# Value products over 64-key halves into two PSUM banks, and scores as three products of split queries and keys

## The chip, the cores and the metric

The kernel runs on one core of one Trainium2 chip. The metric is the device time of one execution in microseconds (us), lower is better. Two kernels are told apart by medians of several executions of each on the same chip.

## What is computed

Inputs are q, k and v for 8 batches, 12 heads, 448 positions and 64 values per head, two 12x12 matrices that mix heads, and the weights of a gated feed-forward. All is float32.

```python
scores = scale * np.matmul(q, k.transpose(0, 1, 3, 2))
scores = np.einsum('bhij,hg->bgij', scores, w_pre)
scores = scores - np.max(scores, axis=-1, keepdims=True)
attn = np.exp(scores)
attn = attn / (np.sum(attn, axis=-1, keepdims=True) + 1e-09)
attn = np.einsum('bhij,hg->bgij', attn, w_post)
attn_out = np.matmul(attn, v)
# x = attn_out as 3584 rows of 768
h = (x @ w1) * (x @ w2) @ w3
out = h @ w_out
```

w_pre and w_post mix the twelve heads at each pair of positions, so scores of all heads have to stand side by side on partitions for the mixing, and the attention has to come back to one head at a time for the product with v.

## The kernel before

The attention of the eight batches runs in 360 steps: a step `n` stands for 10 query rows (`IB`) of a batch, 45 steps per batch (`NB`). All engines work through one program written in the order of the steps (the loop from L889); each engine takes its own instructions in that order, and every DMA is issued from SP's queue. In the order of a step:

- `do_later` (L927) issues the stores put off by the step before, after `fetch` (L926, even steps) has asked for mixed rows of scores; `load_kq` (L933) asks for queries and keys six steps ahead of their use.
- `largest` (even steps, DVE) takes the minimum of the mixed scores for `exp`; `scale` (odd steps) prepares w_post over the sums.
- `pieces` or `unit_pieces` (L950 to L960) convert float64 words of the weights to float32 pairs.
- `advance` (L968, L972) issues a share of the feed-forward's products (`e`, `eg`, `eo`), which fill TensorE between the attention's products.
- `exp` (even steps, ACT), then `av` (L974), `post` and `mix` (odd steps), and last one score unit, `qk` (L982).

**Scores** (`qk`, L166). A unit is a pair of heads `p` and 128 query rows `c` (two pairs and 64 rows each for c = 3). Two 64-row blocks times two heads make four products of 64 rows by 64 columns of weights with 448 keys moving, in float32. On the chip a float32 product is two matmul records. The four take the four quadrants of the array. The two PSUM banks (0 and 1) are copied by ACT (L179, L180) to `st` and stored to `raw_d`.

**Values** (`av`, L292). When 15 steps (150 query rows, the last time 148) of mixed attention stand in `mt`, six pairs of heads `g` are multiplied with v, three at a step and three two steps later. The 448 keys stand in four blocks (`NJ`) of 128; of the last block only 64 keys exist, and in `mt` the other half is zero: for every head, the first 5 of 10 query rows hold their 64 keys on the lower partitions and the other 5 on the upper. A product has 128 rows and 64 columns, two beside each other for the two heads. The result is gathered in bank 0 (`psa`); for batches from 2 on (`ONE`), ACT copies it to `xd` (L308) and it is stored to `x_d`. Batches 0 and 1 go another way (L321).

**Ends.** `ends` holds the closures that empty PSUM banks; `bank(i)` runs them before it hands out a bank that is still to be emptied. The score unit of the step uses banks 0 and 1 right after `post` and `mix`.

**Words.** `ask_words` (L96) loads words ahead into the pool `cs`, five buffers with tag `s` (`DEEP`), and `converting` (L132) uses one per piece: ACT squares it (L110), four DVE operations make float32 (L121 to L124), and in a later piece ACT and POOL split it in two parts (L129, L130), which are stored (L425). The first 40 words belong to a fold of two weights in batch 0, the next 32 to w1 and w2 around batch 1. In a piece the loads ahead are asked for first, then the current word is converted, then the one before is split. The same buffers serve `split` in `sums` (L483) later on.

Feed-forward products use parts of 128x128 weights in `fp32r`, which is one matmul record per product; three products (`PAIRS`) of high and low parts make one float32 product.

## Time and profile before

| what | us |
|---|---|
| median of 3 runs | 1441.87 |
| lowest and highest run | 1441.68 and 1443.87 |
| the profiled execution, whole | 1437.83 |
| its span, from the first instruction to the last | 1436.1 |

A busy TensorE is shown by PE and its weight loads by PEld; DVE, ACT, POOL and SP are the other engines. A row of a group gives operation, shapes, count, then busy us and the mean ns of one, then the idle time of the engine ahead of them. Matmuls are pipelined: one starts before the one before has ended, so their pace is read from start to start. A row of a timeline merges instructions of one line: start of the first, time from it to the end of the last, and their count.

### The profile page before, as it was taken

The numbers are of one execution on the slowest core, as the hardware profiler recorded it, in microseconds if no ns is written. First come the engines' busy times: TensorE is split into PE (matmuls) and PEld (weight loads), VectorE is DVE, ScalarE is ACT, GpSimd is POOL, SyncE is SP. The second block draws the span as 40 slices with busy tenths as digits, with TensorE's granted clock in tenths as the row PEclk, the third lists the DMA queues.
The fourth block names the chain that finished last, engine by engine and source line by source line (L and its number), as shares of the span: only waits on it lengthen the run. The fifth ranks groups of instructions, "written<-read, shape, count | busy, mean of one in ns | idle before, by whom it ended". The sixth has DMA issues, their size and how long they took to land.

```text
span 1436.1 us, 45775 instructions
## 1 busy us (share of the span) xinstructions
PE 1382.4 (96%) x18684; PEld 1055.2 (73%) x18684; DVE 741.1 (52%) x1497; ACT 832.4 (58%) x1952; POOL 620.3 (43%) x754
## 2 busy tenths in 40 slices
PE   5889999999999999999999999999999999999998
PEld 2457786776677667776777777777777777899988
DVE  6867566767544544432444436334444446345563
ACT  4867666777766666665656556556555445422231
POOL 2433233434433544532345336334335446446693
PEclk7989999999999999999999999999999999999999
DMA  8998789999999999999989979799879757698775
GB/s 294 366 326 279 236 270 322 320 312 317 324 286 348 355 356 330 362 346 349 287 275 290 320 259 280 249 323 354 288 229 281 241 177 223 195 337 270 231 232 171
DMA packets 203761, 416.87 MB, mean 290 GB/s; under 512 B 20528, under 2 KB 120112, under 8 KB 203472
## 3 DMA queue, kind: packets, MB, share of 16 engines
q1 hardware_dynamic: 203552, 413.94, 87.6%
q8 instruction: 149, 2.44, 0.7%
q14 instruction: 60, 0.49, 0.1%
HBM read 279.77 MB, written 134.09 MB: 288 GB/s over the span
## 4 chain that ended last, share of the span: by engine, by line
PE 82%; DMA 8%; DVE 4%; ACT 2%; issue 1%; POOL 1%; SPq 0%; DVEq 0%; POOLq 0%; ACTq 0%
PE e L702 21%; PE psa L301 11%; PE pso L260 10%; PE psm L220 9%; PE psq L174 7%; PE eg L522 5%; PE psf L360 4%; PE eo L553 4%; PE e2o L702 4%; PE e1o L702 4%; PE e3o L702 4%; DMA wu<-w_d 3%; DMA r<-raw_d 2%; DMA raw_d<-st 2%; ACT e L235 1%
## 5 line engine op out<-in xcount | busy, mean ns | idle before, releaser
L247 POOL TENSOR_SCALAR w<-wpo,ri 128x60 f32<-128x60 f32 x360 | 180.7, 518 | 485.1 <-DVE ri L245 465.3
L227 DVE TENSOR_REDUCE mn<-psm 128x1 f32<-128x448 f32 x360 | 207.7, 618 | 321.6 <-PE psm L220 321.3
L274 ACT COPY mt<-pso 128x480 f32<-128x480 f32 x352 | 197.9, 621 | 185.8 <-PE pso L260 185.6
L702 PE MATMUL e<-eh,wu 128*128 128x448 f32 x1008 | 296.8, 371 | 6.4 <-DVE c L656 3.2
L235 ACT ACTIVATE e<-psm,mn 128x448 f32<-128x448 f32 x360 | 226.8, 643 | 7.9 <-DVE mn L227 7.9
L702 PEld LDWEIGHTS e<-eh,wu 128*128 128x128 f32 x1008 | 187.5, 188 | 52.2 <-issue 26.8
L260 PEld LDWEIGHTS pso<-w,e 60*64 60x64 f32 x10080 | 175.2, 135 | 51.0 <-issue 42.5
L220 PE MATMUL psm<-r,wsc 60*64 60x448 f32 (+1 forms) x1440 | 191.2, 550 | 19.1 <-DVE cx L124 8.3
L260 PE MATMUL pso<-w,e 60*64 60x60 f32 x10080 | 199.1, 224 | 0.4 <-ACT mt L274 0.3
L702 PE MATMUL e<-el,wu 128*128 128x448 f32 x504 | 186.9, 371 | 0.0
L301 PE MATMUL psa<-mt,v 128*64 128x150 f32 (+1 forms) x2304 | 156.9, 292 | 4.1 <-ACT st L179 4.1
L301 PEld LDWEIGHTS psa<-mt,v 128*64 128x64 f32 x2304 | 143.6, 137 | 20.1 <-ACT st L179 6.7
L174 PE MATMUL psq<-kq 64*64 64x448 f32 x1176 | 154.6, 542 | 2.4 <-ACT st L179 2.4
L656 DVE TENSOR_TENSOR c<-c,e 128x448 f32<-128x448 f32 x168 | 101.7, 618 | 87.7 <-PE e L702 82.9
L179 ACT COPY st<-psq 128x448 f32<-128x448 f32 x162 | 86.4, 533 | 73.7 <-ACT mt L274 34.1
L522 PE MATMUL eg<-xh,wu 128*128 128x448 f32 x384 | 119.2, 381 | 6.3 <-DMA wu<-w_d 6.3
L641 POOL TENSOR_TENSOR el<-x,eh 128x448 fp32r<-128x448 f32 x90 | 103.7, 1170 | 32.8 <-ACT eh L640 29.9
L702 PEld LDWEIGHTS e<-el,wu 128*128 128x128 f32 x504 | 94.6, 188 | 22.5 <-issue 14.1
L174 PEld LDWEIGHTS psq<-kq 64*64 64x64 f32 x1176 | 60.8, 135 | 56.4 <-issue 28.8
L522 PEld LDWEIGHTS eg<-xh,wu 128*128 128x128 f32 x384 | 71.9, 190 | 38.7 <-issue 24.0
L244 DVE TENSOR_SCALAR sa<-sm 128x2 f32<-128x2 f32 x180 | 34.9, 194 | 113.6 <-ACT e L235 113.1
L180 ACT COPY st<-psq 128x448 f32<-128x448 f32 x162 | 87.6, 541 | 0.0
(99 smaller groups left out, 2010.1 us busy)
## 6 DMA issues: line engine op xcount, KB each, us to landing
r<-raw_d SPq DMA_DIRECT2D x344, 210.0 KB, 5.1
raw_d<-st SPq DMA_DIRECT2D x138, 448.0 KB, 6.1
wu<-w_d SPq DMA_DIRECT2D x104, 384.0 KB, 6.7
wu<-s_d SPq DMA_DIRECT2D x96, 384.0 KB, 4.8
wu<-w_d SPq DMA_DIRECT2D x51, 512.0 KB, 5.5
kq<-kq SPq DMA_DIRECT2D x42, 448.0 KB, 7.0
wu<-s_d SPq DMA_DIRECT2D x36, 512.0 KB, 4.9
x<-x_d SPq DMA_DIRECT2D x72, 224.0 KB, 5.7
```

Of the source, the lines that this page charges most:

```text
L174: nc.tensor.matmul(ps[s][z * PP:(z + 1) * PP], t[rows, q:q + PP], t[rows, k:k + S], start=True, stop=True)
L220: nc.tensor.matmul(ps[s][c * PP:(c + 1) * PP, :S], self.wsc[k], r[k, c], start=True, stop=True)
L227: self.nc.vector.tensor_reduce(mn[:, s:s + 1], self.psm[m][s][:, :S], axis=AX.X, op=ALU.min)
L235: nc.scalar.activation(e, p[:, :S], AF.Exp, bias=mn[:, s:s + 1], scale=-1.0, accum_out=sm[:, s:s + 1])
L247: nc.gpsimd.tensor_scalar_mul(w2[:, s], self.wpo, ri[:, s:s + 1])
L260: nc.tensor.matmul(self.pso[c][z * PP:(z + 1) * PP, at:at + HK], e[k, j * PP:(j + 1) * PP], w2s[k, s], start=True, stop=True)
L274: self.nc.scalar.copy(dst.rearrange("p j g (s i) -> p j s g i", s=2), src)
L301: nc.tensor.matmul(self.psa[rows, g % 3, :W], v[:, j, rows], mt[:, j, 2 * g + s, :W], start=(j == 0), stop=(j == NJ - 1))
L522: nc.tensor.matmul(p, u[:, k % (K1 // 2), x], xs[y][:, k], start=(k == 0 and t == 0), stop=(k == K1 - 1 and t == 2))
L641: nc.gpsimd.tensor_tensor(lo, x, hi.bitcast(F32), op=ALU.subtract)
L656: nc.vector.tensor_tensor(a[out], a[to[0]], p, op=ALU.add)
L702: nc.tensor.matmul(p, w[:, k, x], ops[m, k][y], start=(k == 0 and t == 0), stop=(k == nk - 1 and t == 2))
```

## The change

From batch 2 on, `av` takes keys in halves of 64: four products, two heads times two halves, stand in the four quadrants of the array, the halves going to banks 0 and 1. Of the last block each half is multiplied only with the query rows whose keys it holds (`halves`, half the columns). ACT copies bank 0 to `xd` and DVE adds bank 1.

From pair 2 of batch 2 on, `split_kq` makes a high and a low part of queries and keys (ACT `kh`, POOL `kl` in two halves), three steps before a pair's first unit. A score unit with c < 3 is then three products of parts per head, 64 rows by 128 columns in `fp32r`, six matmul records where there were eight. The unit with c = 3 stays as it was and moves ahead of its two pairs; both pairs' loads are asked for six steps before it.

The parts take memory: the pool of words is 3 buffers from the 41st word on, with two further buffers that live until the fold is over; `ask_words` then keeps 2 words asked for, not 5. `split` in `sums` uses 3 buffers. The host puts the last 64 query rows in front.

TensorE at the first score unit of batch 3, pair 0, before: `psm` are the mixed scores, `psq` the banks of the unit (the last figure but one is the head), `kq` queries and keys, `eg` a feed-forward product.

```order
L220 MATMUL psm43_0_4878<-r43_4697,wsc_138 64x448
L220 MATMUL psm43_1_4879<-r43_4697,wsc_138 64x448
L174 MATMUL psq3_0_0_0_4886<-kq3_0_4495 64x448
L174 MATMUL psq3_0_0_1_4887<-kq3_0_4495 64x448
L174 MATMUL psq3_0_0_0_4886<-kq3_0_4495 64x448
L174 MATMUL psq3_0_0_1_4887<-kq3_0_4495 64x448
L522 MATMUL eg0_4_1_4752<-xh0_1260,wu19_4729 128x448 x2
```

And after, `kh` and `kl` being the high and the low part:

```order
L242 MATMUL psm44_0_5020<-r44_4838,wsc_138 64x448
L242 MATMUL psm44_1_5021<-r44_4838,wsc_138 64x448
L189 MATMUL psq3_0_0_0_5028<-kh3_0_4866 128x448
L189 MATMUL psq3_0_0_1_5029<-kh3_0_4866 128x448
L189 MATMUL psq3_0_0_0_5028<-kl3_0_4867,kh3_0_4866 128x448
L189 MATMUL psq3_0_0_1_5029<-kl3_0_4867,kh3_0_4866 128x448
L189 MATMUL psq3_0_0_0_5028<-kh3_0_4866,kl3_0_4867 128x448
L189 MATMUL psq3_0_0_1_5029<-kh3_0_4866,kl3_0_4867 128x448
L563 MATMUL eg0_5_0_4965<-xl0_1261,wu20_4835 128x448
```

Four products of 64 output rows, two records each, became six of 128 output rows; the unit has stayed between the mixing and the feed-forward.

TensorE in the value products of batch 2, before (`mt` the attention, `v` a pair of heads):

```order
L301 MATMUL psa2_0_0_5984<-mt2_0_5258,v2_0_5280 64x150 x8
L301 MATMUL psa2_0_0_5984<-mt2_0_5258,v2_1_5282 64x150 x8
L301 MATMUL psa2_0_0_5984<-mt2_0_5258,v2_2_5284 64x150 x8
L260 MATMUL pso0_141<-w253_5885,e53_0_5864 64x60
L260 MATMUL pso1_142<-w253_5885,e53_0_5864 64x60
```

And after, the end of the first pair of heads and the start of the second; the last figure but one of `psa` is the bank:

```order
L333 MATMUL psa2_0_0_0_6074<-mt2_0_5318,v2_0_5342 64x150
L333 MATMUL psa2_0_0_1_6075<-mt2_0_5318,v2_0_5342 64x150
L341 MATMUL psa2_0_0_0_6074<-mt2_0_5318,v2_0_5342 64x15x5
L341 MATMUL psa2_0_0_1_6075<-mt2_0_5318,v2_0_5342 64x15x5
L341 MATMUL psa2_0_0_0_6074<-mt2_0_5318,v2_0_5342 64x15x5
L341 MATMUL psa2_0_0_1_6075<-mt2_0_5318,v2_0_5342 64x15x5
L333 MATMUL psa2_0_0_0_6074<-mt2_0_5318,v2_1_5344 64x150
L333 MATMUL psa2_0_0_1_6075<-mt2_0_5318,v2_1_5344 64x150
```

Eight products a pair became twelve over three blocks and four at half the columns for the last block.

The queue of SP in batch 1, where words of w1 and w2 are converted, before: `cs` is a load of words, `w_d` a store of a converted unit `wu`, `r` a fetch of scores, `raw2` a store of scores.

```order
L425 DMA w0_d_70<-wu13_4182 128x768
L103 DMA cs59_4215<-w2 128x3x256
L202 DMA r39_4273<-raw1_d_63 60x2x448 x2
L188 DMA raw2_d_64<-st2_4_2_4267 128x896
L425 DMA w1_d_71<-wu14_4270 128x768
L103 DMA cs60_4281<-w1 128x3x256
L425 DMA w1_d_71<-wu15_4308 128x768
L103 DMA cs61_4323<-w1 128x3x256
```

And after:

```order
L466 DMA w0_d_70<-wu13_4209 128x768
L105 DMA cs56_4242<-w1 128x3x256
L224 DMA r39_4302<-raw1_d_63 60x2x448 x2
L210 DMA raw2_d_64<-st2_4_1_4296 128x896
L466 DMA w1_d_71<-wu14_4299 128x768
L105 DMA cs57_4310<-w1 128x3x256
L466 DMA w1_d_71<-wu15_4342 128x768
L105 DMA cs58_4357<-w2 128x3x256
```

Behind the store of unit 13 word 59 was asked for, and now word 56. On ACT the squares (`cm`) of words stand as before, one per piece:

```order
L112 ACTIVATE cm55_4244<-cs55_4153 128x384
L296 COPY mt1_1_3780<-pso0_141 128x4x2x12x5
L296 COPY mt1_1_3780<-pso1_142 128x4x2x12x5
L201 COPY st2_4_1_4296<-psq2_4_1_0_4288 128x448
L202 COPY st2_4_1_4296<-psq2_4_1_1_4289 128x448
L131 CAST wu14_4299<-cx54_4157 128x3x128
L112 ACTIVATE cm56_4312<-cs56_4242 128x384
```

Word 56, which is asked for in the piece that squares word 55, is the next word that ACT takes.

The diff, its changed lines alone:

```diff
...
-DEEP = 5
+DEEP, KEPT = 5, 3
+PARTED = (2, 2)
...
-        while len(self.asked) < depth and self.sources:
+        while len(self.asked) < (depth if self.n_words < 5 * KF else KEPT - 1) and self.sources:
-            s = self.cs.tile([128, CW, 2], I32, tag="s", name=f"cs{n}", bufs=DEEP)
+            kept = n % DEEP < KEPT or n >= 5 * KF
+            s = (self.cs if kept else self.fp).tile([128, CW, 2], I32, tag="s", name=f"cs{n}", bufs=KEPT if kept else DEEP - KEPT)
...
+    def split_kq(self, b, p):
+
+        x = self.kqs[b, p][:, PP:]
+        n = 2 * S - PP
+        hi = self.kh.tile([128, n], F32R, tag="kh", name=f"kh{b}_{p}")
+        lo = self.kp.tile([128, 2 * S], F32R, tag="kq", name=f"kl{b}_{p}", bufs=4)[:, :n]
+        self.nc.scalar.copy(hi, x)
+        for half in (slice(0, n // 2), slice(n // 2, n)):
+            self.nc.gpsimd.tensor_tensor(lo[:, half], x[:, half], hi[:, half].bitcast(F32), op=ALU.subtract)
+        self.kqs[b, p, "parts"] = hi, lo
+
-        return [(self.kqs[b, p], j * PP, S) for p, j in pairs]
+        return [(self.kqs[b, p], (j + 1) * PP % S, S) for p, j in pairs]
-        for z, (t, q, k) in enumerate(self.parts(b, p, c)):
-            for s in range(2):
-                rows = slice(s * D, (s + 1) * D)
-                nc.tensor.matmul(ps[s][z * PP:(z + 1) * PP], t[rows, q:q + PP], t[rows, k:k + S], start=True, stop=True)
+        if c < 3 and (b, p) >= PARTED:
+            t = self.kqs[b, p, "parts"]
+            for n, (x, y) in enumerate(PAIRS):
+                for s in range(2):
+                    rows = slice(s * D, (s + 1) * D)
+                    nc.tensor.matmul(ps[s], t[x][rows, c * QT:(c + 1) * QT], t[y][rows, 3 * QT:],
+                                     start=(n == 0), stop=(n == 2))
+        else:
+            for z, (t, q, k) in enumerate(self.parts(b, p, c)):
+                for s in range(2):
+                    rows = slice(s * D, (s + 1) * D)
+                    nc.tensor.matmul(ps[s][z * PP:(z + 1) * PP], t[rows, q:q + PP], t[rows, k:k + S],
+                                     start=True, stop=True)
...
+    def halves(self, w, z):
+
+        n = w // IB
+        yield lambda t: t[:, :n * IB].rearrange("p (u s i) -> p u s i", s=2, i=IH)[:, :, z]
+        if w % IB:
+            yield lambda t: t[:, n * IB + z * IH:min(n * IB + (z + 1) * IH, w)]
+
-            self.psa = self.bank(0, f"psa{b}_{a}_{g}")[:, :3 * GB * IB].rearrange("p (g i) -> p g i", g=3)
+            self.psa = [self.bank(z, f"psa{b}_{a}_{g}_{z}")[:, :3 * GB * IB].rearrange("p (g i) -> p g i", g=3)
+                        for z in range(1 + (b >= ONE))]
-        for j in range(NJ):
+        for j in range(NJ - (b >= ONE)):
-                nc.tensor.matmul(self.psa[rows, g % 3, :W], v[:, j, rows], mt[:, j, 2 * g + s, :W],
-                                 start=(j == 0), stop=(j == NJ - 1))
+                for z, psa in enumerate(self.psa):
+                    keys = slice(z * PP, (z + 1) * PP) if b >= ONE else slice(0, 128)
+                    nc.tensor.matmul(psa[rows, g % 3, :W], v[keys, j, rows], mt[keys, j, 2 * g + s, :W],
+                                     start=(j == 0), stop=(j == NJ - 1), skip_group_check=b >= ONE)
+        if b >= ONE:
+            for s in range(2):
+                rows = slice(s * D, (s + 1) * D)
+                for z, psa in enumerate(self.psa):
+                    keys = slice(z * PP, (z + 1) * PP)
+                    for part in self.halves(W, z):
+                        nc.tensor.matmul(part(psa[rows, g % 3]), v[keys, NJ - 1, rows], part(mt[keys, NJ - 1, 2 * g + s]),
+                                         start=False, stop=True, skip_group_check=True)
-            q, dst = self.psa[:, :, :W], self.x_d[b][g // 3][:, :, cols]
+            (q, r), dst = (t[:, :, :W] for t in self.psa), self.x_d[b][g // 3][:, :, cols]
+                nc.vector.tensor_tensor(x, x, r, op=ALU.add)
-            self.ends.append((0, leave))
+            self.ends += [(0, leave), (1, lambda: None)]
-            q = self.psa[:, :, :W]
+            q = self.psa[0][:, :, :W]
...
-            s = self.cs.tile([128, CW, 2], I32, tag="s", name=f"s{w}_{f}_{m}", bufs=DEEP)
+            s = self.cs.tile([128, CW, 2], I32, tag="s", name=f"s{w}_{f}_{m}", bufs=KEPT)
...
-        loads, qks, avs = {}, {}, {}
+        loads, qks, avs, splits = {}, {}, {}, {}
-            units = [(b, p, c) for g in range(0, HP, 2) for p, c in [*itertools.product((g, g + 1), range(3)), (g + 1, 3)]]
+            units = []
+            for g in range(0, HP, 2):
+                three = [*itertools.product((g, g + 1), range(3))]
+                units += [(b, *x) for x in ([(g + 1, 3), *three] if (b, g) >= PARTED else [*three, (g + 1, 3)])]
-                if c == 0:
-                    loads.setdefault(max(n - 6, 0), []).append((b, p))
+                if (b, p) < PARTED:
+                    if c == 0:
+                        loads.setdefault(max(n - 6, 0), []).append((b, p))
+                elif c == 3:
+                    loads.setdefault(n - 6, []).extend([(b, p - 1), (b, p)])
+                elif c == 0:
+                    splits[n - 3] = b, p
...
+                self.kh = self.pool("kh", 2, side="right")
...
+            if n in splits:
+                self.split_kq(*splits[n])
...
-    kq = np.ascontiguousarray(np.stack([qt.reshape(B, HP, 2 * D, S), kt], axis=3))
+    qr = qt.reshape(B, HP, 2 * D, S)
+    kq = np.ascontiguousarray(np.stack([np.concatenate([qr[..., 3 * QT:], qr[..., :3 * QT]], axis=3), kt], axis=3))

```

## Prediction

> **What bounds the kernel now.** I read the page first, then the windows, the waits of TensorE, the groups by form, and timelines of a step.
>
> ```profile
> span 1436.1 us, 45775 instructions
> PE 1382.4 (96%) x18684; PEld 1055.2 (73%) x18684; DVE 741.1 (52%) x1497; ACT 832.4 (58%) x1952; POOL 620.3 (43%) x754
> PE   5889999999999999999999999999999999999998
> ```
>
> After the first tenth TensorE is busy nearly all the time. Windows (PE, PEld, DVE, ACT and POOL busy us with counts, then clock, DMA share and GB/s) for the conversion of w1 and w2 and for all of the steps in which values of batches 2 to 7 are made:
>
> ```profile
> 220.00:375.00 155.00, 149.18 (x2406) 105.00 (x2397) 110.17 (x235) 116.27 (x278) 62.76 (x84) 1.00 0.95 318
> 400.00:1260.00 860.00, 846.82 (x12535) 646.79 (x12532) 382.33 (x815) 511.48 (x1206) 373.89 (x471) 1.00 0.89 291
> ```
>
> In the second TensorE works 98% of the time and ACT 59%, so that a product saved there is time saved. In the first ACT is at 75% and the DMA engines at 95%, and there TensorE already waits for ACT's `exp`; these are its waits from 190 to 400 us (total, times, longest):
>
> ```profile
> PE psm L220 <- ACT e L235: 5.2, 8, 1.4
> ```
>
> So two places decide: TensorE's own pace from 400 us on, and whether ACT is held up before 400 us.
>
> **Value products.** A step of batch 3 on TensorE, and the groups by form (mean ns of one last ahead of the idle time):
>
> ```profile
> 700.49 0.36 PE L702 MATMUL e<-el,wu 128*128 128x448 f32 x1
> 700.78 3.28 PE L301 MATMUL psa<-mt,v 128*64 128x150 f32 x48
> 703.99 1.08 PE L260 MATMUL pso<-w,e 60*64 60x60 f32 x55
> ...
> 704.86 0.98 PE L220 MATMUL psm<-r,wsc 60*64 60x448 f32 x7
> 705.61 0.98 PE L174 MATMUL psq<-kq 64*64 64x448 f32 x8
> 706.52 0.67 PE L702 MATMUL e<-eh,wu 128*128 128x448 f32 x2
> 707.03 0.37 PE L702 MATMUL e<-el,wu 128*128 128x448 f32 x1
> 707.24 0.57 PE L702 MATMUL e<-eh,wu 128*128 128x448 f32 x2
> 707.64 0.36 PE L702 MATMUL e<-el,wu 128*128 128x448 f32 x1
> ```
>
> ```profile
> L260 PE MATMUL pso<-w,e 60*64 60x60 f32 x10080 | 199.1, 224 | 0.4 <-ACT mt L274 0.3
> L301 PE MATMUL psa<-mt,v 128*64 128x150 f32 x1536 | 105.0, 293 | 3.4 <-ACT st L179 3.4
> ```
>
> The 48 value records take 3.28 us; less the last one's 0.29 they are 24 rounds of two, 0.130 us each. The mixing's 8 records (the first is merged into another row) take 0.75 us to the start of the scores: two rounds of four, 0.375 us for 448 columns, so four quadrants do run beside each other, and 150 columns should keep 0.13 us a round. Three pairs of heads then take 18 rounds of four at 0.130 and 6 at half the columns, 0.065: 2.73 us where 24 rounds took 3.12, 0.39 less. With 148 columns the halves are 70 columns and, apart, 5 and 3. The smallest products shown are those of L260: 55 in 1.08 less 0.22 us, 0.016 each, 0.063 per round of four. So 18 x 0.128 + 6 x 0.061 + 6 x 0.063 = 3.05 instead of 24 x 0.128 = 3.07, 0.02 less. ACT's copies count the groups:
>
> ```profile
> L308 ACT COPY xd<-psa x36: 528/535/536, 401.5 to 1262.8; 128x450 f32<-128x450 f32 x24, 128x444 f32<-128x444 f32 x12
> ```
>
> 24 x 0.39 + 12 x 0.02 = 9.6 us. Besides, the value products now have the shape of the post products behind them. Today the last value record starts at 700.78 + 2.99 = 703.77 and L260 at 703.99, 0.22 instead of 0.13: 0.09 for the change of shape, which goes 36 times, 3.2 us. Together **-13 us**. The ends: half rounds at 0.10, midway to a full one, and nothing from the shape, 24 x 0.18 = -4; and a pace of 0.125 as well, -17.
>
> DVE's sum must end before the scores take bank 1. In the same step the copy and DVE's next work stand here, and the nearest sum of 448 columns:
>
> ```profile
> 704.11 0.53 ACT L308 COPY xd<-psa 128x450 f32<-128x450 f32 x1 [2.19 <-PE psa L301]
> 705.87 1.16 DVE L227 TENSOR_REDUCE mn<-psm 128x1 f32<-128x448 f32 x2 [4.49 <-PE psm L220]
> L656 DVE TENSOR_TENSOR c<-c,e 128x448 f32<-128x448 f32 x168 | 101.7, 618 | 87.7 <-PE e L702 82.9
> ```
>
> DVE has been idle for 4.49 us. The sum runs from 704.64 to 705.3, the scores start at 705.61 (0.1 sooner in the new order): 0.2 us to spare. Queued behind it is `largest`, which waits for the mixing until 705.87 anyway. **0 us**; where DVE is late, at most its 0.62 us in 24 of the 36 cases, some +7.
>
> **Score products.** Six records in three rounds of two replace eight in two rounds of four. A feed-forward product of the same 448 columns in `fp32r` takes 0.20 us (two from 707.24 to 707.64), so three rounds take 0.61 instead of 0.75: -0.14. But the shape now differs from the mixing's, too. What a change costs is to be read behind the scores: from 705.61 to 707.03 are 1.42 us, of which 0.75 are scores and 0.40 two products; 0.27 stay, in which TensorE drains, some 0.06 of offset between quadrants ends, and the first weights of 128 columns come late. Into the value products it is 0.09 (0.29 from 700.49 to 700.78, less 0.20). For the new change ahead of the scores I take 0.2, the row with 128 columns of weights without the offset: +0.06 a unit. Units: 6 batches of 18, less the 6 of the two pairs before pair 2 of batch 2, 102. **+5 us**; with 0.09 it is -5, and with no cost at all -14.
>
> Here the Trainium skill speaks against the change: TensorE: Matmul & The Clock Gate, Part 3, "Measured speedup vs the span model", gives 3.07 for four row tiles, not 4. Taken for two tiles (1.54), an estimate, three rounds would take 0.79 us and the scores +24 instead of +5. The mixing's two rounds in 0.75 us say otherwise.
>
> The units with c = 3 move ahead of their pairs with the same products, copies and stores, on the same queues. On SP's queue two loads of queries and keys now stand together, ahead of a fetch of scores:
>
> ```profile
> kq<-kq SPq DMA_DIRECT2D x42, 448.0 KB, 7.0
> r<-raw_d SPq DMA_DIRECT2D x344, 210.0 KB, 5.1
> ```
>
> The loads are asked for six steps ahead, some 24 us at 1436 / 360 = 4 us a step, and the fetches four, 16 us; both cover 7.0 + 5.1. **0 us**; uncovered, a fetch would be late by one load, 7 us, at most 17 times, which nothing here points to.
>
> **The splits.** 34 pairs get one ACT copy of 832 columns and two POOL subtractions of 416; nearest are casts and subtractions of 448:
>
> ```profile
> L640 ACT CAST eh<-x x90: 560/570/614, 663.0 to 1348.5; 128x448 fp32r<-128x448 f32 x90
> L641 POOL TENSOR_TENSOR el<-x,eh x90: 1127/1148/1636, 663.7 to 1353.3; 128x448 fp32r<-128x448 f32 x90
> ```
>
> By columns 1.06 us on ACT and 2.1 on POOL. From 400 us on ACT and POOL (43%) have room, and w2, queued on POOL behind them, is used two steps later: nothing. Without that cover it would be 27 ACT copies, 29 us. Seven stand ahead of the last word in the new order, where ACT is the tight engine: **+2**, between 0 and 7.
>
> **The words.** This is the term that decides. Squares of words on ACT, and loads of words on SP's queue:
>
> ```profile
> 239.13 0.56 ACT L110 ACTIVATE cm<-cs 128x384 f32<-128x384 f32 x1 [1.53 <-DVE cx L124]
> 243.48 0.58 ACT L110 ACTIVATE cm<-cs 128x384 f32<-128x384 f32 x1
> 248.00 0.57 ACT L110 ACTIVATE cm<-cs 128x384 f32<-128x384 f32 x1
> 243.48 0.40 SPq L103 DMA_DIRECT2D cs<-w  x1
> ```
>
> A load is issued as the square of its piece starts, 4.4 us before the next. Five buffers gave it four such gaps; with two words asked for it has one. Its landing (min, median, max) and the windows that these are from, 186 to 230 and 230 to 275 us:
>
> ```profile
> DMA to landing us min/median/max: 4.9/5.3/5.6
> 186.00:230.00 44.00, 43.34 (x698) 34.81 (x696) 25.14 (x56) 28.02 (x68) 10.89 (x18) 1.00 0.87 275
> DMA to landing us min/median/max: 7.1/7.2/8.3
> 230.00:275.00 45.00, 42.69 (x679) 30.10 (x677) 33.65 (x72) 34.10 (x84) 18.01 (x25) 1.00 1.00 341
> ```
>
> ACT takes its work in order: while a square waits for its word, `exp`, copies and all else wait behind it, and TensorE for `exp`. The next load is issued when ACT reaches the waiting square, not when that is done, so two pieces take a latency and a gap: (4.4 + 5.3) / 2 = 4.85 us a piece, 0.45 more, or (4.4 + 7.2) / 2 = 5.8, 1.4 more. Pieces and how ACT waited in 220 to 375 us:
>
> ```profile
> L110 ACT ACTIVATE cm<-cs 128x384 f32<-128x384 f32 x31 | 17.6, 569 | 8.7 <-DVE cx L124 8.7
> ACT xh L322 <- PE psa L301: 14.2, 7, 2.8
> ```
>
> Of 31 pieces 24 follow closely; seven value groups between them let ACT catch up. 24 x 0.45 = 11 us, 24 x 1.4 = 34. As the stretch slows its DMA load falls towards the window with 0.87, so I take the lower latency, less some 0.4 us regained at each of the seven: **+8 us**, ends 0 and 27.
>
> **Split buffers of the sums.** Three for five; their stores:
>
> ```profile
> L483 ACT CAST s<-y x44: 513/530/640, 424.1 to 624.6; 128x384 fp32r<-128x384 f32 x32, 128x512 fp32r<-128x512 f32 x12
> ```
>
> A cast every 4.6 us on average, so a buffer comes round after 13.7 us; a store, like the loads, lands within 5 to 8. Only bunched casts wait: **+2**, ends 0 and 8.
>
> **The rivals.**
> - The words arrive in time. If the landing falls to the gap of 4.4 us, or TensorE's queue holds enough to bridge the rest, words and splits cost 0 and -13 + 5 + 2 = -6 stays: 1436. For it: it is one load per gap and the latency has been 4.9 at times. Against it: the median was above 4.4 in both windows. It decides at 4.4 us.
> - The words cost their full latency of 7.2 us: 27 for 8, +23: 1465. For it is the DMA share of 1.00; against it, that the stretch slows.
> - No price for the shape ahead of the scores: -14 for +5, so -15: 1427. Against it, both changes of shape that the step shows have a price.
> - Half-array `fp32r` products don't overlap: three rounds become six, 102 x 0.61 = 62 us more, 1508. Against it, the mixing. By the Trainium skill's 3.07 above (TensorE: Matmul & The Clock Gate) it would be 1465.
>
> **How the numbers follow.** -13 + 5 + 0 + 2 + 8 + 2 = +4 us. The profiled execution took 1437.83 us (span 1436.1 and 1.7 around it), 4.0 below the median of the runs, 1441.87; runs are compared by medians, so 1441.87 + 4 = **1446 us**. Its own range, words between 5 and 18, is 1443 to 1456; chance 0.40. Words in time 0.28, full latency 0.12, free shape 0.13, no overlap 0.07. The range 1425 to 1465 leaves out the last, half of the full latency's and a tail of the free shape's.
>
> A measurement of this kernel can tell 0.2%, 2.9 us. Faster by that: words in time 0.25, free shape 0.12, forecast 0.02, together 0.39. Slower: forecast 0.27, full latency and no overlap 0.19, together 0.46. Within: 0.15.
>
> **What would show it.** Right: from 220 to 400 us ACT waits at L112 for DMA `cs`, at a period near 4.9 us, and TensorE's wait for `exp` grows from 5.2 us to over 10; a value group of 150 columns takes 2.75 us; scores start 0.2 us late behind the mixing and last 0.61 us. Wrong: no waits for `cs`; score rounds of 0.4 us; a wait of L189 for DVE's sum; value rounds above 0.13 us.

## The result and the profile after

The changed kernel takes 1492.03 us (median of 4 runs, 1491.03 to 1495.78); the kernel before took 1442.53 on the same chip. The ratio is 1.035, with an interval of 1.0331 to 1.0369: 50 us slower. The forecast was 1446 us with a range of 1425 to 1465, so the result lies far outside it. The profiled execution has a span of 1489.9 us, 53.8 more than before.

The page of after: span, busy time, TensorE's busy tenths and the tenths of its granted clock.

```profile
span 1489.9 us, 49560 instructions
PE 1402.5 (94%) x20496; PEld 1070.2 (72%) x20496; DVE 784.6 (53%) x1533; ACT 859.7 (58%) x1986; POOL 694.8 (47%) x822
PE   5789998988899999999999999999999999999999
PEclk7989998999999999999999999999999999999999
```

A slice is 37 us. Slices 7 and 9 to 11, between 223 and 410 us, fall below nine tenths. To place the loss, the start of the n-th mixing (its first `psm` record) of the after trace was set against that of the same mixing before:

```
before at us    204    249    319    389    507    793    811   1200   end
after later by  0.7    9.7   20.3   34.5   44.8   46.2   52.1   54.4  53.8
```

So 34 us are lost while w1 and w2 are converted, 10 up to 507 us, 6 between 793 and 811 us, and nothing is won back behind. The same two windows as before (busy us with counts of PE, PEld, DVE, ACT, POOL, then clock, DMA share, GB/s):

```profile
220.00:375.00 155.00, 135.58 (x1985) 93.10 (x1984) 96.72 (x198) 102.95 (x240) 63.03 (x81) 0.92 0.84 270
...
400.00:1260.00 860.00, 829.93 (x13809) 630.41 (x13811) 416.63 (x844) 531.69 (x1232) 423.86 (x515) 0.99 0.90 290
```

In the first TensorE is busy for 87% where it was 96, ACT for 66% where it was 75, and the DMA share fell from 0.95 to 0.84: each waits for another. The waits from 190 to 420 us (total, times, longest), and the landing of the words (min, median, max):

```profile
ACT cm L112 <- DMA cs<-w: 34.2, 20, 5.0
...
PE psm L242 <- ACT e L257: 17.3, 10, 2.7
...
PE pso L282 <- ACT mt L296: 4.4, 2, 2.6
```

```profile
DMA to landing us min/median/max: 3.7/5.2/6.0
```

ACT stands at a square for its word, and TensorE for `exp`: 17.3 us where it was 5.2. What holds the next word up stands on SP's queue, of which these are the longest waits for POOL in the same stretch, before and after:

```profile
SPq L425 <- POOL wu L130: 31.5, 27, 2.3
```

```profile
SPq L466 <- POOL wu L132: 61.5, 29, 6.4
```

22 of 30 loads of words go out right behind such a store of a converted unit, 0.4 us after it. The store waits for POOL's part of the unit, and that for ACT's cast (L131), which stands on ACT behind a square. So a late word holds up the next load.

ACT's timeline at the second to fourth of its waits for a word, and TensorE's clock some microseconds before (window row as above, clock third from the end):

```profile
238.47 0.55 ACT L112 ACTIVATE cm<-cs 128x384 f32<-128x384 f32 x1 [4.99 <-DMA cs<-w]
...
241.16 0.55 ACT L112 ACTIVATE cm<-cs 128x384 f32<-128x384 f32 x1 [0.73 <-DMA cs<-w]
...
245.37 0.55 ACT L112 ACTIVATE cm<-cs 128x384 f32<-128x384 f32 x1 [1.25 <-DMA cs<-w]
```

```profile
233.00:236.40 3.40, 3.40 (x13) 1.73 (x12) 0.76 (x3) 0.48 (x2) 1.81 (x3) 0.54 0.95 345
...
280.00:290.00 10.00, 10.00 (x163) 7.00 (x161) 6.29 (x11) 6.65 (x15) 2.97 (x4) 1.00 0.91 296
```

In the first window only 13 records start in 3.4 us. TensorE is shown as busy, but its clock is half. The clock of the after trace has eight such stretches of 3.4 us and three of 6.8 from 220 us on, 48 us in all; before had one of 3.4. Each of them begins within 3.3 us of the end of a stop of TensorE, or in it: the longest distance from one matmul's start to the next there is 1.85 to 3.06 us. Six other stops of 1.82 to 2.77 us behind 220 us were not followed by one.

A value group and, elsewhere, a score unit behind its mixing in the timeline:

```profile
585.78 1.00 PE L333 MATMUL psa<-mt,v 64*64 64x150 f32 x24
586.60 0.32 PE L341 MATMUL psa<-mt,v 64*64 64x75 f32 x8
586.74 0.94 PE L333 MATMUL psa<-mt,v 64*64 64x150 f32 x24
...
588.55 1.03 PE L282 MATMUL pso<-w,e 60*64 60x60 f32 x55
```

```profile
769.88 0.97 PE L242 MATMUL psm<-r,wsc 60*64 60x448 f32 x7
770.79 0.47 PE L189 MATMUL psq<-kh 64*128 64x448 f32 x2
771.10 0.37 PE L189 MATMUL psq<-kl,kh 64*128 64x448 f32 x2
771.30 0.37 PE L189 MATMUL psq<-kh,kl 64*128 64x448 f32 x2
771.60 0.67 PE L743 MATMUL e<-eh,wu 128*128 128x448 f32 x2
```

The group takes 2.77 us from 585.78 to the post products at 588.55, where it took 3.21: the quadrants work as forecast. The first two score records now need 0.31 us to the next, the others 0.20, and 0.30 to the feed-forward.

But from 420 to 1290 us TensorE's waits hold rows that the kernel before did not have, waits for which the profile knows no releaser ("issue"):

```profile
PE pso L282 <- issue: 9.7, 7, 2.8
PE psm L242 <- issue: 4.2, 2, 2.5
...
PE eo L594 <- issue: 1.1, 1, 1.1
...
PE psq L189 <- issue: 0.5, 1, 0.5
PE psa L333 <- issue: 0.4, 1, 0.4
```

That is 15.9 us. One of these stops, behind a value group of 148 columns; the 6 us between 793 and 811 us in the table are this one and the half clock behind it:

```profile
847.34 0.97 PE L282 MATMUL pso<-w,e 60*64 60x60 f32 x51
851.11 0.36 PE L282 MATMUL pso<-w,e 60*64 60x60 f32 x1 [2.80 <-issue]
851.24 1.89 PE L242 MATMUL psm<-r,wsc 60*64 60x448 f32 x8
```

Ahead of the last of 56 equal post records TensorE stands for 2.8 us, and the mixing behind it takes 1.89 us instead of 0.98, since the clock has fallen.

### The profile page after: what moved, and what is told of

It reads as the page before. It is cut to its first block, busy times and chain, and to the rows that moved or that the text cites. A ratio compares the mean times of both kernels' runs of the same rounds, so it can differ in the third digit from the quotient of the medians.

```text
span 1489.9 us, 49560 instructions
## 1 busy us (share of the span) xinstructions
PE 1402.5 (94%) x20496; PEld 1070.2 (72%) x20496; DVE 784.6 (53%) x1533; ACT 859.7 (58%) x1986; POOL 694.8 (47%) x822
## 3 DMA queue, kind: packets, MB, share of 16 engines
q8 instruction: 163, 2.67, 0.7%
## 4 chain that ended last, share of the span: by engine, by line
PE 74%; DMA 11%; DVE 4%; issue 4%; ACT 4%; POOL 2%; SPq 1%; DVEq 0%; ACTq 0%; POOLq 0%
PE e L743 19%; PE pso L282 9%; PE psm L242 8%; PE psa L333 8%; PE psq L189 5%; PE eg L563 4%; PE psf L401 4%; PE e1o L743 4%; PE e2o L743 4%; PE e3o L743 3%; PE eo L594 3%; DMA cs<-w 3%; PE psq L195 2%; DMA wu<-w_d 2%; ACT e L257 2%
## 5 line engine op out<-in xcount | busy, mean ns | idle before, releaser
L269 POOL TENSOR_SCALAR w<-wpo,ri 128x60 f32<-128x60 f32 x360 | 175.6, 506 | 379.5 <-DVE ri L267 361.7
L242 PE MATMUL psm<-r,wsc 60*64 60x448 f32 (+1 forms) x1440 | 204.5, 565 | 34.5 <-ACT e L257 20.1
L282 PEld LDWEIGHTS pso<-w,e 60*64 60x64 f32 x10080 | 178.4, 135 | 59.4 <-issue 52.4
L333 PE MATMUL psa<-mt,v 64*64 64x150 f32 (+3 forms) x3168 | 143.8, 291 | 4.6 <-ACT st L201 4.1
L333 PEld LDWEIGHTS psa<-mt,v 64*64 64x64 f32 (+1 forms) x3168 | 116.2, 134 | 20.9 <-issue 7.7
L563 PE MATMUL eg<-xh,wu 128*128 128x448 f32 x384 | 122.2, 390 | 4.2 <-DMA wu<-w_d 4.2
L170 POOL TENSOR_TENSOR kl<-kq,kh 128x416 fp32r<-128x416 f32 x68 | 78.0, 1167 | 81.2 <-ACT kh L168 81.2
L266 DVE TENSOR_SCALAR sa<-sm 128x2 f32<-128x2 f32 x180 | 46.7, 259 | 120.0 <-ACT e L257 119.3
L242 PEld LDWEIGHTS psm<-r,wsc 60*64 60x64 f32 (+1 forms) x1440 | 53.9, 137 | 50.0 <-ACT e L257 30.4
```

Source lines behind the costliest of these rows:

```text
L242: nc.tensor.matmul(ps[s][c * PP:(c + 1) * PP, :S], self.wsc[k], r[k, c], start=True, stop=True)
L269: nc.gpsimd.tensor_scalar_mul(w2[:, s], self.wpo, ri[:, s:s + 1])
L282: nc.tensor.matmul(self.pso[c][z * PP:(z + 1) * PP, at:at + HK], e[k, j * PP:(j + 1) * PP], w2s[k, s], start=True, stop=True)
L333: nc.tensor.matmul(psa[rows, g % 3, :W], v[keys, j, rows], mt[keys, j, 2 * g + s, :W], start=(j == 0), stop=(j == NJ - 1), skip_group_chec ...
L563: nc.tensor.matmul(p, u[:, k % (K1 // 2), x], xs[y][:, k], start=(k == 0 and t == 0), stop=(k == K1 - 1 and t == 2))
```

## The experiments

The theory after the result had three parts: words that come late, whose waits pass to TensorE whole and drop its clock; value products that are faster but make TensorE stop; scores that cost a little. The rivals were a loss from the score products or the splits, and a value part that is slower in itself. Ratios are against the kernel before on the same chip (1444.97 us for e1 to e4, 1443.72 for e5 to e8, 1444.38 for e9 to e11). A time with + or - behind a ratio is worked out from that ratio; the difference of the medians is mostly within 1.3 us of it, but 12.5 for 10.2 in e6 and 41.2 for 37 in e8. Waits, stops and clocks are each read from one profiled run.

### Words and buffers alone (e1_words_only)

```diff
-DEEP = 5
+DEEP, KEPT = 5, 3
-        while len(self.asked) < depth and self.sources:
+        while len(self.asked) < (depth if self.n_words < 5 * KF else KEPT - 1) and self.sources:
...
-            s = self.cs.tile([128, CW, 2], I32, tag="s", name=f"s{w}_{f}_{m}", bufs=DEEP)
+            s = self.cs.tile([128, CW, 2], I32, tag="s", name=f"s{w}_{f}_{m}", bufs=KEPT)
```

> The kernel before with nothing but the words' memory taken away: 3 buffers and 2 words asked for from the 41st word on, and 3 buffers for the splits of the sums. Theory (the words' lead holds up ACT before 400 us, TensorE's clock drops with it, and the buffers of the sums hold ACT up a little after that): 30 to 42 us slower, ACT's squares waiting for loads of words for 25 to 40 us, half-clock stretches between 220 and 410 us. Rival (the stretch is slow because of the new ACT copies of queries and keys and the doubled loads there, which this kernel doesn't have): under 15 us slower.

1472.87 us, ratio 1.0191 (1.015 to 1.0231): +27.6 us, over half of the whole loss with no product changed. Expected were 30 to 42 us and waits of 25 to 40, so the loss is below and the waits are above what was expected. From 190 to 420 us:

```profile
ACT cm L111 <- DMA cs<-w: 46.3, 21, 5.9
...
PE psm L221 <- ACT e L236: 11.1, 8, 2.8
PE pso L261 <- ACT mt L275: 7.3, 4, 2.8
```

TensorE waits 18.4 us for ACT, and in this stretch its clock is at half for 31 us.

### Two words asked, with all five buffers (e2_lead_only)

```diff
-        while len(self.asked) < depth and self.sources:
+        while len(self.asked) < (depth if self.n_words < 5 * KF else KEPT - 1) and self.sources:
```

> The kernel before with five buffers as they were, but only 2 words asked for from the 41st word on. Theory (it is the lead and not the number of buffers that matters for the words): 28 to 38 us slower, and all of it before 400 us; what the kernel with 3 buffers loses beyond this one, 0 to 8 us, belongs to the sums' splits from 420 to 640 us. Rival (the third buffer is what is missing, because a load waits for its buffer): within 10 us of the kernel before.

1468.12 us, ratio 1.0156 (1.0112 to 1.0201): +22.5, below the 28 to 38 that were expected. Memory is as before, so the lead of the loads alone makes most of it; the sums' three buffers and the rest of e1 are some 5 us more, though the two intervals overlap.

### Three words asked (e5_lead_three)

As e2, with `KEPT = 4`, so that three words are asked for and a load has two gaps of 4.4 us.

> The kernel before with 3 words asked for from the 41st word on, five buffers as they were; the kernel with 2 asked for was 22 us slower. Theory (a load has as many gaps of 4.4 us between pieces as words are asked for beyond the first, and lands in 5 to 7 us): with two gaps, 8.8 us, the words come in time again, within 4 us of the kernel before, and ACT waits less than 8 us for loads of words. Rival (every load less in flight costs its share, as five loads fill the DMA engines better): about two thirds of the 22 us, 12 to 17 us slower.

1451.25 us, ratio 1.0044 (1.0026 to 1.0061): +6.3, where at most 4 was expected. The profiled run, 1446.39 us, is one of the two lowest of ten:

```profile
PE psm L220 <- ACT e L235: 8.9, 8, 2.9
...
ACT cm L110 <- DMA cs<-w: 8.4, 4, 3.9
```

And the words' landing:

```profile
DMA to landing us min/median/max: 3.9/5.9/8.2
```

The landing is no shorter than in e2 (5.3 in the median there), but now most words come within the two gaps. A load in flight more takes away 16 of 22.5 us. With one gap, two and four the cost is 22.5, 6.3 and 0, which fits a cost that comes when the gaps don't cover the landing; no run here lies between these points.

### Value products alone (e3_av_only)

The functions `halves`, `av` and its ends as in the change, nothing else.

> The kernel before with the change of the value products alone. The prediction's term: 13 us faster. Theory now (the bursts of more and smaller records from 400 us on run TensorE out of instructions, 13 us of stops that no engine or DMA ends, and its clock drops to half after three of them, 8 us): between 3 us faster and 12 us slower, with some five stops of 1 to 3 us ended by issue in the value groups, the post products behind them or the mixing, and half-clock stretches right behind some of them.

1452.08 us, ratio 1.0056 (1.0032 to 1.008): +8.1, where the shorter groups should have given -11. The stops are here too, from 420 to 1290 us:

```profile
PE pso L260 <- issue: 9.6, 5, 2.4
...
PE psq L174 <- issue: 3.4, 2, 1.9
...
PE psm L220 <- issue: 1.7, 1, 1.7
```

So 14.7 us of stops and the clock behind them belong to the value products, and neither words nor scores are needed for them.

### Only the last block in halves (e4_av_tail)

The first three blocks stay products of 128 keys, two beside each other (36 records a group); the last block's four quadrants for all three pairs stand together behind them (24 records, half the columns).

```diff
-        for j in range(NJ):
+        for j in range(NJ - (b >= ONE)):
...
+        if b >= ONE and g % 3 == 2:
+            for i in range(g - 2, g + 1):
...
+                            nc.tensor.matmul(part(psa[rows, i % 3]), self.vs[b, i][keys, NJ - 1, rows], part(mt[keys, NJ - 1, 2 * i + s]),
+                                             start=(z == 1 and i == g - 2 and n == 0), stop=True, skip_group_check=True)
```

> The kernel before with other value products: the first three blocks of keys as 128-row products as they were, and behind the three pairs of heads the last block alone in quadrants of 64 keys and half the columns, into two banks; DVE adds the second bank's half of the columns. 60 records a group of 150 columns where the kernel before has 96 and the changed one 96 and more (96 of 64 rows). Theory of the stops: with fewer records no stop ended by issue, and the whole saving shows, 18 rounds of 0.130 and 6 of 0.065 instead of 24 of 0.130 and one change of shape less: 8 to 13 us faster. Rival (stops come from the quadrants or the second bank, not from the number of records): stops as in the kernel with the value change alone.

1438.28 us, ratio 0.9956 (0.9933 to 0.9979): 6.4 us faster than before, the best version here, though 8 to 13 was expected. The group of 150 columns takes 2.93 us, 0.28 less, which 24 times is 6.7. Its only stop without a releaser:

```profile
PE pso L260 <- issue: 0.4, 1, 0.4
```

It has 60 records a group, where the change has 96. (The expectations of this run and of e6 give 96 records a group for the kernel before; its trace has 48.)

### As many records in the old form (e6_av_split)

Each value product of before is cut in two by columns: 96 records a group, two beside each other, half the columns each.

```diff
-                nc.tensor.matmul(self.psa[rows, g % 3, :W], v[:, j, rows], mt[:, j, 2 * g + s, :W],
-                                 start=(j == 0), stop=(j == NJ - 1))
+                for x in (slice(0, W // 2), slice(W // 2, W)) if b >= ONE else (slice(0, W),):
+                    nc.tensor.matmul(self.psa[rows, g % 3, x], v[:, j, rows], mt[:, j, 2 * g + s, x],
+                                     start=(j == 0 and x.start == 0), stop=(j == NJ - 1), skip_group_check=b >= ONE)
```

> The kernel before with every value product from batch 2 on in two of half the columns: the same shapes, bank and columns, but 192 records a group where there were 96, and 36 groups. Theory (TensorE runs out of instructions in a burst of many records, whatever their shape): stops ended by issue of 1 to 3 us in or behind the value groups, 10 us or more in all, and 10 to 25 us slower. Rival (the stops come with the quadrants or the second bank): no stop ended by issue over 1 us, and 0 to 5 us slower, for 24 more rounds a group at some 2.5 ns each and the smaller records.

1456.18 us, ratio 1.0071 (1.005 to 1.0092): +10.2. The stops were expected at 10 us or more, and are 2.7:

```profile
PE pso L260 <- issue: 2.7, 3, 2.2
```

So the count of records alone doesn't make them. The time lies in the range that was expected, but not for the reason that was given. The groups are slower (3.36 us for 3.21, 3.30 for 3.17: 24 x 0.15 + 12 x 0.13 = 5 us), which makes 96 records come at 29 per us, not at 35 as in e3. The theory of the count fell here; what stayed was how fast the records follow each other.

### Where the stops come from

TensorE's program itself comes in packets of a DMA queue of its own. The page's rows of it (packets, MB, time), before and after:

```profile
q8 instruction: 149, 2.44, 0.7%
```

```profile
q8 instruction: 163, 2.67, 0.7%
```

That is 2.67 MB / 163 = 16.4 KB, and 20496 / 163 = 126 matmul records, a packet. The number of packets follows TensorE's records in the other runs too: 149 for 18684 before, 154 for 19404 in e4, 164 for 20700 in e3, 125 to 126 records each. With its weight loads, semaphore and drain rows the after trace has 41693 rows of TensorE, 256 a packet. For every stop by "issue" from 420 to 1290 us with over 1.2 us between two matmul starts, the end of the stop and how long before it a packet of this queue started:

```
after   ends at  439.9 484.7 540.0 851.1 1012.4 1068.9
        packet    2.36  2.56  2.29  2.46   2.37   2.61 us before
e3      ends at  507.3 550.3 607.3 645.3 810.6 917.9 977.7 1028.2
        packet    2.53  2.65  2.33  2.43  2.41  2.40  2.27   2.34
e6      ends at  652.0       e10  ends at  556.8
        packet    2.52            packet    2.30
```

Sixteen of sixteen start 2.27 to 2.65 us ahead of the record that goes on, while stops for a weight or a fetch stand in no such order (in before: 0.62, 3.04 and three with no packet in the 4 us ahead). The place in the program says the same. Counted over all rows of TensorE in order of their start, the rows ahead of the record that goes on leave a remainder of 193, divided by 256, in each of the sixteen: all of them stand at the same place of a packet, as its edge would. The five stops of that length in before leave 166, 75, 179, 255 and 125. So TensorE waits for its own next instructions, and goes on some 2.4 us after their packet starts. The packet itself takes 0.9 to 1.3 us of that; what fills the rest, no run here shows.

### Feed-forward products between value group and post products (e9_spread, e10_av_spread, e11_tail_spread)

If the supply of instructions is too slow for a dense stretch, a pause of long products in it should end the stops. Half of the feed-forward products of the step ahead of a value group go behind it; e9 does this in the kernel before, e10 in e3, e11 in e4.

```diff
             for x in avs.get(n, []):
                 self.av(*x)
+            advance(after.get(n, 0))
...
+        after = {n: share[n - 1] // 2 for n in avs if n > LATE}
+        for n, x in after.items():
+            share[n - 1] -= x
```

> The kernel before, with half of the feed-forward products that stand ahead of each value group of batches 2 to 7 (6 or 7 products, some 1.3 us of TensorE) moved behind it, between the value group and the post products. The control for the next two. Nothing is added, and TensorE is busy either way, so both theories expect no change beyond 3 us. A value group starts 1.3 us closer to the score unit of an earlier step, whose banks it needs; if ACT has not emptied them by then TensorE waits, at most some 0.5 us a group in 36, up to +9 us with half of the groups beside a score unit.

1460.24 us, ratio 1.0102 (1.0075 to 1.0129): +14.7, where no more than 3, and 9 at worst, was expected. Two reasons show in its trace. TensorE's shape now changes twice more: 0.22 us from the value group into the feed-forward products, whose first record takes 0.31 instead of 0.20, and 0.30 out of them into the post products, against 0.22 straight from values to post. That is 0.22 + 0.11 + 0.30 - 0.22 - 0.20 = 0.21 us, 7.6 us for 36 groups. And its clock is at half for 31 us (3 before), each time at a stop of TensorE of 1.6 us or more. How far the new order causes those stops was not settled.

> The value part of the change alone (96 to 120 records a group, run earlier: +8.1 us, 14.6 us of stops of TensorE for which the profile shows no releaser), with the same move of feed-forward products between the group and the post products. Theory: the stops come where too many short records follow each other (the group and the 56 post records at once, about 150 to 180 in 3.8 us), since TensorE's own instructions arrive too slowly; with 1.3 us of long products between the two, the stops fall from 14.6 to under 5 us and the time comes from +8 to between -10 and 0 against before. Rival: the stops come from the number of records in all, wherever they stand, or from the four-quadrant form itself: stops of 10 us and more stay, time +4 to +12.

1456.30 us, ratio 1.008 (1.0051 to 1.0109). With nearly as many instruction packets (164) and the same records as e3, the stops fell from 14.7 us to 1.9:

```profile
PE pso L260 <- issue: 1.2, 2, 0.8
...
PE psq L174 <- issue: 0.7, 1, 0.7
```

So the stops need both the many records and their density; the four quadrants alone don't make them. The time against before missed the expected -10 to 0, because the move itself costs 14.7. Against its control the value part is now 3 to 4 us faster, by ratios and by medians, where e3 was 8 slower than its own; the groups give 24 x (3.21 - 2.88) - 12 x 0.10 = 6.7 and the rest of the stops takes 1.9. The intervals of e9 and e10 overlap, so the gain in time is likely and not shown; the fall of the stops is read from one trace of each.

> The best version so far (only the last block of each pair of heads in halves, 60 to 84 records a group, -6.4 us before) with the same move. Theory: it had stops of only 0.4 us, so the move has nothing to gain: within 2 us of -6.4 plus what the control shows. Rival (some of its gain was still lost to stops that the one profile happened not to show): a further 3 us or more below the control's share.

1453.55 us, ratio 1.0068 (1.0041 to 1.0094): 6.7 us below the control by medians and 4.9 by ratios, where e4 is 6.4 below before. It is what was expected: the tail form had no stops to lose.

### Scores from batch 5 on, words as before (e7_scores_late)

With the score products and splits of the change only from pair 2 of batch 5 (`PARTED = (5, 2)`), 48 units and 16 splits, memory allows five words ahead.

> The kernel before with the change of the scores alone, from pair 2 of batch 5 on, 16 splits and 48 units, the words as before (the memory for the parts is free by then). The prediction's term, 0.05 us a unit for the change of shape ahead of the scores less what the three rounds save: 2 to 4 us slower, the mixing's last record to the first of the scores 0.47 us, and three rounds of 0.2 to 0.3. Rival (the splits' copies and subtractions are not hidden on ACT and POOL): 16 splits at 0.3 to 0.6 us more, 7 to 13 us slower, with TensorE waiting for ACT or POOL from 900 us on.

1446.04 us, ratio 1.0015 (1.0 to 1.0029): +2.2. It agrees with +0.06 a unit (48 x 0.06 = 2.9) and with hidden splits.

### Scores and words, old value products (e8_no_av)

All of the change but `av`.

> The changed kernel with its value products as they were: scores, words and buffers changed. If the parts simply add, 50 us less the 8 that the value products cost alone: 42 us slower than before, of which words and buffers 27, scores 5 and 10 open. Theory of the words: the open 10 us lie before 500 us, where copies and subtractions for the parts stand on ACT and POOL beside late words, with TensorE's clock at half for longer. Rival: they lie behind 500 us, with the scores' units and splits.

1484.89 us, ratio 1.0257 (1.0215 to 1.0299): +37. One of its four runs is 10 us below the other three; the medians give +41. There is no stop by "issue" at all from 420 to 1290 us. With e3's 8 the parts make 45 of the 50 us, by medians 48. Scores and splits are 37 - 27.6 = 9.4 beside e1: about 5.4 are the units (next section), the rest is near the intervals' width. In the traces e8 is 35.3 us late at the mixing at 389 us and e1 30.2, so the copies and loads for the parts may cost some 5 us in the stretch where words are converted.

## Why the prediction was wrong

**Words, +8 (ends 0 and 27): the step that failed first.** Alone they cost 27.6 with the buffers and 22.5 without, so the size was off, at the upper end. (That end doesn't follow from its own step: 34 less seven times 0.4 is 31, not 27.) It wasn't the latency: the landing was 5.2 us in the median, and 5.3 had been taken. The failing step is "two pieces take a latency and a gap ... 0.45 more" together with the 0.4 us "regained at each of the seven" value groups. The squares of the 31 pieces went from 222.8 to 374.7 us before and from 223.5 to 408.1 after: 32.7 us more over 30 gaps, 1.1 each, not 0.45. By that step every second piece would have waited, 0.9 us each; ACT waited at 20 squares, 1.7 us each. From the issue of its load to its square a word took 6.25 us in the median, with the landing 5.2. Two things make the difference. While ACT waits for a word, `exp`, copies and the cast of the unit before wait behind it, so TensorE, the mixing and the next `exp` are late as well, and so are POOL's part, the store on SP's queue and the load behind that store: SP's wait there went from 31.5 to 61.5 us. The prediction let the next load go when ACT reaches the waiting square; it went 0.2 us (median) before that square began, when the wait was over. And TensorE's clock: its waits for ACT grew by 17.3 + 4.4 - 5.5 = 16 us in this stretch, and 31 us at half clock cost up to 15 more (an estimate: half of the stretch, were TensorE never waiting in it). Together that is up to 31 of the 34 us. The same sum, waits and half of the slow stretch, gives 28 of the 30 us that e1's trace has lost at the mixing at 389 us, and 26 of 26 in e2's. The prediction had no term for the clock, though it counted on stops.

**Value products, -13 (ends -4 and -17): right on what it reckoned, wrong on what it left out.** 24 x (3.21 - 2.77) + 12 x 0.02 = 10.8 us of TensorE's time are saved, near the 12.8 forecast, shape and all; the 2.75 us for a group came out as 2.77. What was missed is that 96 to 120 records follow each other in the time of 48, with 56 more behind them, and outrun the supply of instructions. Stops of 14.7 us and the clock behind them turned -11 into +8. This is the second step that failed: fewer rounds were taken for less time, and the instructions that the rounds need were put at nothing. No rival named it: the only danger weighed was that quadrants don't overlap.

**DVE's sum, 0: right.** No wait of TensorE names it.

**Score products, +5: right in size, by luck in its parts.** (0.06 x 102 is 6.1; the prediction entered 5.) From the mixing's last record to the second feed-forward product a unit takes 1582 ns where it took 1529 (medians): 0.053 x 102 = 5.4 us. The way there was different: scores start 0.15 us later behind the mixing's last record (466 ns, 312 before), not 0.2, their records take 0.07 more, not 0.14 less, and the feed-forward products follow 0.17 sooner (293 ns, 463 before). By the prediction's estimate from the Trainium skill (TensorE: Matmul & The Clock Gate, Part 3, "Measured speedup vs the span model", 3.07 for four row tiles) it would have been +24; e7 and this pace speak against that for this case.

**Splits, +2, and the sums' buffers, +2: not contradicted, and not settled alone.** ACT waited 7.1 us for stores of the sums from 420 to 640 us; e1 less e2 gives 5, inside the ends 0 and 8. The 10 us lost between 389 and 507 us are not theirs: 3.7 are lost from the mixing at 445.9 us to the next, and 6.5 from that at 498.1 us to the next, and in these two stand the instruction stops that end at 484.7 and 540.0 us in after, with 3.4 and 6.8 us at half clock behind them.

**The rivals.** Full latency gave the right price for the words, 27, by a wrong cause: the landing did not rise to 7.2. Words in time is refuted by 34.2 us of waits at L112; no price for the shape and no overlap are refuted by the score unit and the group. The range failed since it held the words' upper end without the value part's reverse. Of the signs named ahead, the waits at L112, a wait for `exp` of over 10 us, the group and, with 0.15 us for 0.2, the late scores came true. The period of the squares, 4.9, was 5.98 in the median (4.59 before), and the scores took 0.81 us to the next product, not 0.61 (0.91 before).

**What stays open:** some 5 of the 50 us. Put together from the after trace, the 34.5 us at 389 us, 15.9 of stops, half of 17.1 less 3.4 us at half clock behind it, -10.8 for the values, +5.4 for the scores and 2.6 less in TensorE's other waits make 49 of the 53.8 (an estimate). How the loss up to 389 us divides between words and the parts' own copies was not measured alone.

## What to carry to other kernels

A load whose lead shrinks to about its latency isn't priced by the mean shortfall: on an in-order engine that feeds the bound one, each late arrival stops that one too, and then its clock. Count the records of a dense stretch, not only its time: when small products are packed closer, find the queue that carries instructions in the profile, and ask how many records a packet holds and how long one takes. Take the part of a packing that removes work with few new records (here the half-empty last block, -6.4 us) before the part that splits everything.

## What the hardware showed that was not expected

**Instructions arrive late.** Sixteen stops, 1.3 to 3.1 us from one matmul's start to the next, end 2.27 to 2.65 us after a 16 KB packet of the instruction queue starts, all at the same place in a packet. The Trainium skill, Runtime: NRT & Kernel Launch, "Instruction fetch mechanics", states blocks of 16 KiB, which the trace confirms, and calls the cost of crossing a boundary mostly hidden. From 420 us on before agrees, with no stop of that kind; after does not, where 150 to 180 matmul records follow each other within 4 us.

**The clock falls after short stops.** All stretches at half clock behind 220 us, but one cut off by the end, last 3.4 us or a multiple, as the Trainium skill states (TensorE: Matmul & The Clock Gate, Part 1, a window of about 3.4 us). But it names an idle window of that length as the cause, and here stops of 1.9 to 3.1 us between matmul starts were enough, though six of 1.8 to 2.8 in the same trace were not. A stop of 2 us can so cost 3.7 (an estimate), since 3.4 us at half clock do the work of 1.7.

**Changes of shape have a price of their own:** 0.09 to 0.2 us each. Moving work between two groups (e9) added two of them to every group, 0.21 us, half of what it cost.
